# Diagonal masks of the first token group by GpSimd, biases as rows, one K block a unit later, output blocks in four PSUM tiles

## The chip, the cores and the metric

One core of a Trainium2 chip runs the kernel: PE (TensorE, matrix products into PSUM), DVE (VectorE), ACT (ScalarE), POOL (GpSimd) and SP (SyncE, whose queue issues every DMA here). The metric is the device time of one execution in microseconds; a time is the median of several executions.

## The reference

A block with conditioned layer norms over x of shape [2048, 512]: first sliding-window attention over the tokens (32 heads of 16, a token sees itself and the 255 before it), then an MLP that mixes tokens (2048 to 1792 to 2048 for every one of the 512 features).

```python
mod = (_silu(c) @ w_mod).reshape(c.shape[0], 6, 1, -1)
sa, ca, ga, sb, cb, gb = (mod[:, n] for n in range(6))
h = _layernorm(x) * (1 + ca) + sa
x = x + ga * A(h, wqkv, wo)        # A: softmax of q k / 4 over 0 <= i - j < 256, times v, @ wo
h = _layernorm(x) * (1 + cb) + sb
x = x + gb * B(h, w1, b1, w2, b2)  # B: layer norm again, gelu(w1^T h + b1), then w2^T u + b2
```

The bias b1 has 1792 elements and b2 2048. In the kernel they are wanted as columns: b1FM holds one of 14 columns of 128 for each block of w1's outputs, b2FM one of 16 for each block of 128 tokens.

## The kernel before, in words

The tokens are cut into 16 blocks of 128 and four groups tg of four blocks. After a short head (loads, first layer norm, the first projections) the attention runs over 96 units `u = (tg, hs, ui)`: four groups, eight half sets of four heads, three units that hold the pieces of keys and queries of one half set (`UNITS`). `ul = 3 * hs + ui` is a unit's place in its group. For unit u the order is written out by hand in one loop (lines 641 to 668) and each engine keeps to it: `emit_exp(u, 0)` on ACT, `emit_scores(u + 1)` on PE, then the matmuls of one "group" (a projection, a transposition, a product with wo) that `plan(tg)` lays at this place, `emit_exp(u, 1)`, `emit_mask(u)` on GpSimd, some steps of layer norms on DVE by a budget of microseconds (`run_dve`), the group's evacuation on DVE, and `emit_av(u - 1)`, the product with V, on PE. A group's PSUM tile "dn" has one buffer, so a group starts after the one before has been evacuated. The score tiles pss have three buffers, two for a unit.

Two masks are applied. On the diagonal blocks (`DIAG`) PE adds -1e9 from `maskD` to the scores, with four matmuls against `identity` at the end of `emit_scores` (line 435). On the far blocks (`FAR`) GpSimd sets the exponentials to zero with `affine_select` (line 457). In group 0 the first unit of a half set (ui = 0) has one block only, its diagonal, and no far mask.

A K projection (`qk_group` with kind "k") is cast by DVE to `ks`, a tile with one buffer (line 265). In group 0 DVE makes the even and odd halves of its first two blocks itself; for all others eight DMAs of 16 KB copy rows of ks into KT (line 275), so the next cast into ks waits until these have landed. `plan` lays the K projections of blocks 2 and 3 of group 0 at ul 5 and 8, the first two of group 1 at ul 18 and 22 of group 0.

All DMAs stand in SP's queue in the order of the program. `later_loads(n)` is called at ul 10 to 17 of group 0: two blocks of zeros for KT, four blocks of wmod, wod, and with n = 7 the two biases, loaded element by element into [128, 14] and [128, 16] tiles (lines 165 and 166). At ul 16 of group 1 DVE casts them to float32 (lines 627, 628), and the space is then used for w1, whose loads follow.

After the attention PE runs the MLP: the first product (lines 717, 804), gelu on ACT, the second product (line 824). For each of four groups of tokens the second product goes into one PSUM tile py of four banks; the last group is ordered by block tl, the others by fc. DVE then makes o1 (line 831) and the output (line 836) of each block, and SP stores it.

Of the kernel before, what the change touches and what calls it, by code (L numbers as in the profile page):

```python
# [8 lines left out]
DT = mybir.dt  # L9
# [3 lines left out]
P = 128  # L13
# [15 lines left out]
def kernel(  # L29
# [52 lines left out]
    bc_gb = const.tile([P, D], DT.bfloat16, name="bc_gb")  # L82
    b1FM = const.tile([P, NF], DT.float32, name="b1FM")
    b2FM = const.tile([P, NT], DT.float32, name="b2FM")

# [17 lines left out]
    c4 = modw.tile([ND, P], DT.bfloat16, name="c4")  # L103
    b1b = modw.tile([P, NF], DT.bfloat16, name="b1b")
    b2b = modw.tile([P, NT], DT.bfloat16, name="b2b")
    sT_rep = modw.tile([P, ND, P], DT.bfloat16, name="sT_rep")
# [44 lines left out]
    nc.gpsimd.memset(ones[:, 1:2], 0.0)  # L151

    def later_loads(n):
        if n < 2:
            dma.dma_start(
                out=Kring[1 + n][:].rearrange("p g n t -> p (g n) t"),
                in_=zero[:].unsqueeze(1).to_broadcast([P, 2 * ND, 4 * P]),
            )
        elif n < 6:
            v = (2, 4, 3, 5)[n - 2]  # L160
            dma.dma_start(out=wmod[:, :, v * D : (v + 1) * D], in_=w_mod_v[:, :, v * D : (v + 1) * D])
        elif n == 6:
            dma.dma_start(out=wod[:], in_=wo_v[:])
        elif n == 7:
            dma.dma_start(out=b1b[:], in_=B_b1.rearrange("(j p) -> p j", p=P))
            dma.dma_start(out=b2b[:], in_=B_b2.rearrange("(j p) -> p j", p=P))

# [110 lines left out]
    def bc_group(v, dst, add1, pool):  # L278
# [14 lines left out]
        return mms, evac, 0.7  # L293

    folded = []
    done = set()
# [30 lines left out]
    with tc.manual_schedule():  # L327
# [86 lines left out]
        def pieces(tg, ui):  # L414
            return [(4 * tg + kb, r0, nr, blk) for kb, r0, nr, blk in UNITS[ui] if 4 * tg + kb >= 0]

        def emit_scores(u):

# [4 lines left out]
            for n, (kb, r0, nr, blk) in enumerate(pieces(tg, ui)):  # L423
                Ksel = (KeT if par == 0 else KoT)[kb // 4][g8]
                k0, q0 = kb % 4 * P, (kb + r0 - 4 * tg) * P
                for j in range(4):
                    rows = slice(32 * j, 32 * j + 32)
                    nc.tensor.matmul(  # L428
                        pss[j // 2][:, j % 2, blk * P : (blk + nr) * P],
                        lhsT=Ksel[rows, k0 : k0 + P], rhs=QT[tg][g8][rows, q0 : q0 + nr * P],  # L430
                        start=(n == 0), stop=False, tile_position=(32 * j, 0), skip_group_check=True,
                    )
            lo, hi = DIAG[ui]
            for j in range(4):
                nc.tensor.matmul(  # L435
                    pss[j // 2][:, j % 2, lo * P : hi * P], lhsT=identity[:],
                    rhs=maskD[:, 0 : hi - lo, :], start=False, stop=True, skip_group_check=True,
                )
# [12 lines left out]
        def emit_mask(u):  # L451
            tg, hs, ui = units[u]
            if tg == 0 and ui == 0:
                return
            et = state[u, "e"]
            lo, hi = FAR[ui]
            nc.gpsimd.affine_select(  # L457
                out=et[:, :, lo * P : hi * P], in_=et[:, :, lo * P : hi * P],
                pattern=[[0, 4], [0, hi - lo], [-1, P]], compare_op=ALU.is_ge, fill=0.0,
                base=-1, channel_multiplier=1,  # L460
            )

# [119 lines left out]
        def plan(tg):  # L582
# [6 lines left out]
            for n in range(1, 4):  # L589
                lay(n - 1, v_group(tg, n, ps_dn))  # L590
            own = ((3, 1, "k"), (4, 1, "q"), (5, 2, "k"), (6, 2, "q")) if tg == 0 else (
                (3, 1, "q"), (4, 2, "k"), (5, 2, "q"))
            for ul, g8, kind in own + ((8, 3, "k"), (9, 3, "q")):
                lay(ul, qk_group(tg, g8, kind, ps_dn))
            if tg == 1:
                for ul, (v, dst, add1) in zip((6, 7, 10, 15), BC):
                    lay(ul, bc_group(v, dst, add1, ps_dn))
                then[6] = [(lambda g=g: fold_wod(g), 0.45, 0) for g in range(ND)]
# [20 lines left out]
        def at_unit(tg, ul, u):  # L619
# [6 lines left out]
            if tg == 1 and ul == 16:  # L626
                nc.vector.tensor_copy(out=b1FM[:], in_=b1b[:])
                nc.vector.tensor_copy(out=b2FM[:], in_=b2b[:])
                modw.release()
# [184 lines left out]
    with tc.tile_pool(name="ftmp", bufs=3) as ftmp, tc.tile_pool(  # L814
        name="ps_y0", bufs=1, space=bass.MemoryType.PSUM
    ) as ps_y0, tc.tile_pool(name="ps_y1", bufs=1, space=bass.MemoryType.PSUM) as ps_y1:
        for tg in range(NT // 4):
            py = (ps_y0, ps_y1)[tg % 2].tile([P, 4, D], DT.float32, name="py")
            order = [(fc, tl) for fc in range(NF) for tl in range(4)]
            if tg == NT // 4 - 1:  # L820
                order.sort(key=lambda x: x[1])
            for fc, tl in order:
                tb = tg * 4 + tl
                nc.tensor.matmul(  # L824
                    py[:, tl, :], lhsT=w2r[:, fc, tb * P : (tb + 1) * P], rhs=guT[fc][:],
                    start=(fc == 0), stop=(fc == NF - 1),
                )
            for tl in range(4):
                tb = tg * 4 + tl
                o1 = ftmp.tile([P, D], DT.bfloat16, name="o1")  # L830
                nc.vector.scalar_tensor_tensor(  # L831
                    out=o1[:], in0=py[:, tl, :], scalar=b2FM[:, tb : tb + 1], in1=bc_gb[:],
                    op0=ALU.add, op1=ALU.mult,
# [35 lines left out]
```

## Time and profile before

| what | value |
|---|---|
| median of 3 runs | 318.99 us (317.1 to 320.08) |
| profiled execution | 318.7 us |
| its span (first to last instruction) | 317.0 us |
| PE busy | 279.4 us (88%) |
| DVE busy | 198.3 us (63%) |
| ACT busy | 194.8 us (61%) |
| POOL busy | 108.8 us (34%) |
| mean granted clock of PE | 0.979 |

The profile is of one execution. Times in it run from the first instruction. A busy share is an average over the whole span: ACT works mostly in the attention (up to about 215 us) and little after it, PE in both, so the stages are read one by one. A granted clock of 1.00 means 2.4 GHz, 0.50 means 1.2 GHz. In a row of the order of time, the bracket at the end gives how long the engine stood idle before the instruction and what released it.

### The profile page before, as it was taken

The numbers are of one execution on the slowest core, as the hardware profiler recorded it, in microseconds if no ns is written. First come the engines' busy times: TensorE is split into PE (matmuls) and PEld (weight loads), VectorE is DVE, ScalarE is ACT, GpSimd is POOL, SyncE is SP. The second block draws the span as 40 slices with busy tenths as digits, with TensorE's granted clock in tenths as the row PEclk, the third lists the DMA queues.
The fourth block names the chain that finished last, engine by engine and source line by source line (L and its number), as shares of the span: only waits on it lengthen the run. The fifth ranks groups of instructions, "written<-read, shape, count | busy, mean of one in ns | idle before, by whom it ended". The sixth has DMA issues, their size and how long they took to land. (4 is left out here: it accounts for less than half of the span.)

```text
span 317.0 us, 7541 instructions
## 1 busy us (share of the span) xinstructions
PE 279.4 (88%) x3125; PEld 133.2 (42%) x3125; DVE 198.3 (63%) x391; ACT 194.8 (61%) x220; POOL 108.8 (34%) x181
## 2 busy tenths in 40 slices
PE   0899689669999989988888998998999999999991
PEld 0544354324545434444444444443444444444440
DVE  5656594306797789988899998997951100405315
ACT  8177688746999997989989799993106311000000
POOL 5132242222355545537665546772620000000000
PEclk9999999957999999999999999999999999999998
DMA  6910049700000346800000000009990000012011
GB/s 202 345 51 0 22 149 311 160 19 15 17 20 3 123 128 202 295 19 9 2 17 19 6 20 16 2 4 312 417 405 24 1 2 0 13 54 68 17 50 66
DMA packets 23307, 28.55 MB, mean 90 GB/s; under 512 B 6888, under 2 KB 18920, under 8 KB 23272
## 3 DMA queue, kind: packets, MB, share of 16 engines
q1 hardware_dynamic: 23272, 28.07, 27.1%
q8 instruction: 24, 0.39, 0.5%
q14 instruction: 11, 0.09, 0.1%
HBM read 22.03 MB, written 2.10 MB: 76 GB/s over the span
## 5 line engine op out<-in xcount | busy, mean ns | idle before, releaser
L446 ACT ACTIVATE et<-pss 128x1024 bf16<-128x1024 f32 (+1 forms) x192 | 172.8, 971 | 24.6 <-PE pss L435 21.9
L457 POOL TENSOR_SCALAR_AFFINE_SELECT et<-et 128x512 bf16<-128x512 bf16 (+1 forms) x88 | 72.0, 818 | 86.8 <-ACT et L446 86.6
L428 PE MATMUL pss<-QT,KT 32*128 32x256 bf16 (+1 forms) x960 | 44.6, 247 | 10.7 <-ACT et L446 6.6
L824 PE MATMUL py<-guT,w2r 128*128 128x512 bf16 x224 | 48.5, 379 | 0.0
L435 PE MATMUL pss<-maskD,identity 128*128 128x128 bf16 (+1 forms) x384 | 45.8, 243 | 0.0
L831 DVE SCALAR_TENSOR_TENSOR o<-py,b2FM,bc_gb 128x512 bf16<-128x512 f32 x16 | 11.3, 746 | 47.9 <-PE py L824 47.9
L474 PE MATMUL po<-et,VaugT 128*32 128x256 bf16 (+1 forms) x960 | 37.9, 252 | 1.3 <-DVE t L488 1.2
L250 PE MATMUL dn<-h1T,wqkv 128*128 128x512 bf16 x128 | 34.3, 394 | 5.3 <-DVE ks L265 2.9
L824 PEld LDWEIGHTS <-w2r 128*128 128x128 bf16 x224 | 21.9, 98 | 26.4
L428 PEld LDWEIGHTS <-KT 32*128 32x128 bf16 x960 | 18.4, 92 | 31.4 <-issue 22.8
L435 PEld LDWEIGHTS <-identity 128*128 128x128 bf16 x384 | 24.7, 98 | 16.0 <-issue 12.1
L474 PEld LDWEIGHTS <-VaugT 128*32 128x32 bf16 x960 | 16.2, 95 | 35.1 <-issue 24.9
L180 POOL TENSOR_TENSOR ln_rstd<-ln_ve,mhalf 128x1 f32<-128x1 f32 (+1 forms) x40 | 24.6, 616 | 3.3
L488 DVE STREAM_TRANSPOSE t<-po 128x512 f32<-128x512 f32 x32 | 22.6, 706 | 2.2 <-PE po L474 2.2
L265 DVE CAST ks<-dn 128x512 bf16<-128x512 f32 x16 | 11.1, 691 | 20.2 <-DMA KT<-ks 12.4
L176 POOL TENSOR_SCALAR ln_ve<-ln_mv 128x1 f32<-128x1 f32 (+1 forms) x40 | 9.8, 246 | 34.7 <-DVE ln_mv L517 13.6
L230 PE MATMUL dn<-wqkv,h1T 128*128 128x512 bf16 x64 | 18.9, 423 | 2.6 <-DVE ks L265 1.5
L250 PEld LDWEIGHTS <-wqkv 128*128 128x128 bf16 x128 | 12.1, 100 | 15.3 <-issue 8.0
L717 PE MATMUL pu<-hb,w1a 128*128 128x512 bf16 x72 | 16.2, 379 | 0.8 <-ACT et L446 0.8
L241 DVE CAST VaugT<-dn 128x512 bf16<-128x512 f32 x15 | 10.3, 685 | 9.7 <-PE dn L230 7.1
L804 PE MATMUL pu<-hb,w1a 128*128 128x512 bf16 x64 | 14.5, 379 | 0.0
L262 DVE CAST QT<-dn 128x512 bf16<-128x512 f32 x15 | 10.3, 685 | 5.2 <-PE dn L250 5.1
(93 smaller groups left out, 267.3 us busy)
## 6 DMA issues: line engine op xcount, KB each, us to landing
w2r<-in_B_w_dram SPq DMA_DIRECT2D x14, 512.0 KB, 10.1
w1a<-in_B_w_dram SPq DMA_DIRECT2D x12, 448.0 KB, 5.2
wmod<-in_w_mod_dram SPq DMA_DIRECT2D x6, 512.0 KB, 8.2
x<-in_A_x_dram SPq DMA_DIRECT2D x16, 128.0 KB, 2.8
KT<-zero SPq DMA_DIRECT2D x2, 1024.0 KB, 8.4
out_dram<-otile SPq DMA_DIRECT2D x16, 128.0 KB, 1.7
KT<-ks SPq DMA_DIRECT2D x112, 16.0 KB, 1.8
w1b<-in_B_w_dram SPq DMA_DIRECT2D x4, 448.0 KB, 6.1
```

The source lines that it names most:

```text
L180: nc.gpsimd.tensor_tensor(out=r[:], in0=ve[:], in1=mhalf[:, 0:n], op=ALU.pow)
L230: nc.tensor.matmul(pv[:], lhsT=h1T[tg][:, dc, tl * P : (tl + 1) * P], rhs=wqkv[:, dc, 2 * D : 3 * D], start=(dc == 0), stop=(dc == ND - 1),)
L250: nc.tensor.matmul(pq[:], lhsT=wqkv[:, dc, col0 : col0 + P], rhs=h1T[tg][:, dc, :], start=(dc == 0), stop=(dc == ND - 1),)
L428: nc.tensor.matmul(pss[j // 2][:, j % 2, blk * P : (blk + nr) * P], lhsT=Ksel[rows, k0 : k0 + P], rhs=QT[tg][g8][rows, q0 : q0 + nr * P], ...
L435: nc.tensor.matmul(pss[j // 2][:, j % 2, lo * P : hi * P], lhsT=identity[:], rhs=maskD[:, 0 : hi - lo, :], start=False, stop=True, skip_gr ...
L446: nc.scalar.activation(out=et[:, 2 * a : 2 * a + 2, b0 * P :], in_=state.pop((u, a))[:, :, b0 * P :], func=ACT.Exp, scale=SCORE_SCALE,)
L457: nc.gpsimd.affine_select(out=et[:, :, lo * P : hi * P], in_=et[:, :, lo * P : hi * P], pattern=[[0, 4], [0, hi - lo], [-1, P]], compare_o ...
L474: nc.tensor.matmul(po[32 * j : 32 * j + 32, q0 : q0 + nr * P], lhsT=VaugT[kb // 4][:, kb % 4, 8 * g8 + 2 * j + par, :], rhs=et[:, j, blk * ...
L488: nc.vector.transpose(out=state["t2"][:, hs % 2, :], in_=state["po"][:])
L717: nc.tensor.matmul(pu[:, i, :], lhsT=w1_of(sc, fc), rhs=hb[sc][:], start=(sc == 0), stop=(sc == NT - 1),)
L804: nc.tensor.matmul(pu[:, i, :], lhsT=w1_of(sc, fc), rhs=hb[sc][:], start=(sc == s0), stop=(sc == NT - 1),)
L824: nc.tensor.matmul(py[:, tl, :], lhsT=w2r[:, fc, tb * P : (tb + 1) * P], rhs=guT[fc][:], start=(fc == 0), stop=(fc == NF - 1),)
```

## The change

Four edits. In group 0, in units with ui 0 or 1 (`late_diag`), the four mask matmuls are left out, the last score matmul closes the sum, and `emit_mask` runs a second `affine_select` on the diagonal block with the sign turned. The biases are loaded as 14 and 16 rows of 128 elements at the start, behind the loads of x; PE transposes these 30 rows as a group at ul 10 of group 0 and DVE copies the result to float32. In every group the projections of block 3 change places: Q at ul 8, K at ul 9. And each output block gets a PSUM tile of its own: two pools of four tiles of one bank, in place of two tiles of four banks.

```diff
-    b1FM = const.tile([P, NF], DT.float32, name="b1FM")
-    b2FM = const.tile([P, NT], DT.float32, name="b2FM")
+    bFM = const.tile([P, NF + NT], DT.float32, name="bFM")
+    b1FM, b2FM = bFM[:, 0:NF], bFM[:, NF : NF + NT]
...
+    b12 = modw.tile([NF + NT, P], DT.bfloat16, name="b12")
...
+    dma.dma_start(out=b12[0:NF, :], in_=B_b1.rearrange("(j p) -> j p", p=P))
+    dma.dma_start(out=b12[NF:, :], in_=B_b2.rearrange("(j p) -> j p", p=P))
...
-        elif n == 7:
-            dma.dma_start(out=b1b[:], in_=B_b1.rearrange("(j p) -> p j", p=P))
-            dma.dma_start(out=b2b[:], in_=B_b2.rearrange("(j p) -> p j", p=P))
...
+    def bias_group(pool):
+        def mms():
+            pb = pool.tile([P, NF + NT], DT.bfloat16, name="dn")
+            nc.tensor.transpose(pb[:], b12[:], identity[0 : NF + NT, 0 : NF + NT])
+            return pb
+
+        def evac(pb):
+            nc.vector.tensor_copy(out=bFM[:], in_=pb[:])
+        return mms, evac, 0.2
...
+        def late_diag(u):
+            tg, hs, ui = units[u]
+            return tg == 0 and ui < 2
...
-                        start=(n == 0), stop=False, tile_position=(32 * j, 0), skip_group_check=True,
+                        start=(n == 0), stop=late_diag(u) and n + 1 == len(pieces(tg, ui)),
+                        tile_position=(32 * j, 0), skip_group_check=True,
...
-            for j in range(4):
+            for j in range(0 if late_diag(u) else 4):
...
-            if tg == 0 and ui == 0:
-                return
             et = state[u, "e"]
-            lo, hi = FAR[ui]
-            nc.gpsimd.affine_select(
-                out=et[:, :, lo * P : hi * P], in_=et[:, :, lo * P : hi * P],
-                pattern=[[0, 4], [0, hi - lo], [-1, P]], compare_op=ALU.is_ge, fill=0.0,
-                base=-1, channel_multiplier=1,
-            )
+            for (lo, hi), sign, on in ((FAR[ui], -1, (tg, ui) != (0, 0)), (DIAG[ui], 1, late_diag(u))):
+                if on:
+                    nc.gpsimd.affine_select(
+                        out=et[:, :, lo * P : hi * P], in_=et[:, :, lo * P : hi * P],
+                        pattern=[[0, 4], [0, hi - lo], [sign, P]], compare_op=ALU.is_ge, fill=0.0,
+                        base=min(sign, 0), channel_multiplier=-sign,
+                    )
...
-            for ul, g8, kind in own + ((8, 3, "k"), (9, 3, "q")):
+            for ul, g8, kind in own + ((8, 3, "q"), (9, 3, "k")):
                 lay(ul, qk_group(tg, g8, kind, ps_dn))
+            if tg == 0:
+                lay(10, bias_group(ps_dn))
...
-                nc.vector.tensor_copy(out=b1FM[:], in_=b1b[:])
-                nc.vector.tensor_copy(out=b2FM[:], in_=b2b[:])
                 modw.release()
...
-        name="ps_y0", bufs=1, space=bass.MemoryType.PSUM
-    ) as ps_y0, tc.tile_pool(name="ps_y1", bufs=1, space=bass.MemoryType.PSUM) as ps_y1:
+        name="ps_y0", bufs=4, space=bass.MemoryType.PSUM
+    ) as ps_y0, tc.tile_pool(name="ps_y1", bufs=4, space=bass.MemoryType.PSUM) as ps_y1:
         for tg in range(NT // 4):
-            py = (ps_y0, ps_y1)[tg % 2].tile([P, 4, D], DT.float32, name="py")
+            pys = [(ps_y0, ps_y1)[tg % 2].tile([P, D], DT.float32, name="py") for tl in range(4)]
...
-                    py[:, tl, :], lhsT=w2r[:, fc, tb * P : (tb + 1) * P], rhs=guT[fc][:],
+                    pys[tl][:], lhsT=w2r[:, fc, tb * P : (tb + 1) * P], rhs=guT[fc][:],
...
-                    out=o1[:], in0=py[:, tl, :], scalar=b2FM[:, tb : tb + 1], in1=bc_gb[:],
+                    out=o1[:], in0=pys[tl][:], scalar=b2FM[:, tb : tb + 1], in1=bc_gb[:],
```

## Rows read from the trace of the kernel before

**Rows 1.** ACT in order of time: start, duration, line, operation, count, idle before.
```profile
36.12 1.94 ACT L446 ACTIVATE et<-pss 128x1024 bf16<-128x1024 f32 x2 [0.98 <-PE pss L435]
40.12 2.49 ACT L446 ACTIVATE et<-pss 128x1024 bf16<-128x1024 f32 x4 [2.06 <-PE pss L435]
...
58.26 3.83 ACT L446 ACTIVATE et<-pss 128x1024 bf16<-128x1024 f32 x4 [0.98 <-PE pss L435]
65.62 1.94 ACT L446 ACTIVATE et<-pss 128x1024 bf16<-128x1024 f32 x2 [3.53 <-PE pss L435]
...
72.91 1.94 ACT L446 ACTIVATE et<-pss 128x1024 bf16<-128x1024 f32 x2 [3.25 <-PE pss L435]
75.97 4.84 ACT L446 ACTIVATE et<-pss 128x1024 bf16<-128x1024 f32 x5 [1.12 <-PE pss L435]
```

**Rows 2.** PE in order of time, 61 to 70 us.
```profile
61.24 0.34 PE L428 MATMUL pss<-QT,KT 32*128 32x256 bf16 x8
64.50 0.69 PE L428 MATMUL pss<-QT,KT 32*128 32x128 bf16 x4 [2.92 <-DMA KT<-ks]
...
69.32 1.01 PE L230 MATMUL dn<-wqkv,h1T 128*128 128x512 bf16 x2 [1.48 <-DVE ks L265]
```

**Rows 3.** DVE in order of time, 53 to 72 us.
```profile
53.74 0.69 DVE L265 CAST ks<-dn 128x512 bf16<-128x512 f32 x1 [2.18 <-PE dn L250]
...
68.58 0.69 DVE L265 CAST ks<-dn 128x512 bf16<-128x512 f32 x1 [9.20 <-DMA KT<-ks]
```

**Rows 4.** SP's queue in order of time, 43 to 66 us.
```profile
43.01 2.59 SPq L155 DMA_DIRECT2D KT<-zero  x2
...
50.89 1.50 SPq L163 DMA_DIRECT2D wod<-in_A_wo_dram  x1
52.43 1.33 SPq L165 DMA_DIRECT2D b1b<-in_B_b_dram  x1
53.80 6.56 SPq L166 DMA_DIRECT2D b2b<-in_B_b_dram  x1
60.47 5.45 SPq L275 DMA_DIRECT2D KT<-ks  x8
```

**Rows 5.** Stretches: busy time of each engine, granted clock, DMA share, GB/s.
```profile
20.00:60.00 40.00, 33.91 (x493) 17.26 (x493) 26.40 (x50) 31.52 (x43) 12.32 (x20) 1.00 0.43 126
...
64.90:74.90 10.00, 8.44 (x66) 3.20 (x67) 3.05 (x5) 5.82 (x6) 1.77 (x2) 0.50 0.08 18
```

**Rows 6.** DMA issues: count, KB each, median us from issue to landing.
```profile
KT<-ks SPq DMA_DIRECT2D x112, 16.0 KB, 1.8
...
wod<-in_A_wo_dram SPq DMA_DIRECT2D x1, 512.0 KB, 10.2
```

**Rows 7.** DMA packets from 59 to 60 us.
```profile
DMA packets 1327, 0.04 MB, mean 36 GB/s; under 512 B 1294, under 2 KB 1327, under 8 KB 1327
```

**Rows 8.** All engines in order of time, 30 to 56 us.
```profile
30.29 0.40 PE L435 MATMUL pss<-maskD,identity 128*128 128x128 bf16 x4
...
30.53 1.03 PE L250 MATMUL dn<-h1T,wqkv 128*128 128x512 bf16 x4
...
37.26 0.69 DVE L265 CAST ks<-dn 128x512 bf16<-128x512 f32 x1 [3.24 <-DMA KT<-ks]
...
38.01 1.02 PE L250 MATMUL dn<-h1T,wqkv 128*128 128x512 bf16 x4 [1.87 <-DVE ks L265]
```

**Rows 9.** All engines in order of time, from 296 us to the end.
```profile
295.68 14.41 PE L824 MATMUL py<-guT,w2r 128*128 128x512 bf16 x66
...
310.12 1.41 DVE L831 SCALAR_TENSOR_TENSOR o<-py,b2FM,bc_gb 128x512 bf16<-128x512 f32 x2 [8.02 <-PE py L824]
...
313.44 0.75 DVE L836 TENSOR_TENSOR otile<-o,x 128x512 bf16<-128x512 bf16 x2
```

**Rows 10.** Groups by line and shape: count, busy us, mean ns, idle before.
```profile
L457 POOL TENSOR_SCALAR_AFFINE_SELECT et<-et 128x512 bf16<-128x512 bf16 x64 | 45.4, 710 | 61.6 <-ACT et L446 61.5
...
L521 DVE TENSOR_SCALAR hb<-h,ln_mv,ln_rstd 128x512 bf16<-128x512 bf16 x12 | 7.0, 587 | 0.0
...
L754 DVE TENSOR_SCALAR hb<-h,ln_mv,ln_rstd 128x512 bf16<-128x512 bf16 x4 | 1.6, 390 | 0.8 <-POOL ln_rstd L180 0.8
```

More of the change, by code (lines that the diff above doesn't have):

```diff
@@ L103 @@
     c4 = modw.tile([ND, P], DT.bfloat16, name="c4")
-    b1b = modw.tile([P, NF], DT.bfloat16, name="b1b")
-    b2b = modw.tile([P, NT], DT.bfloat16, name="b2b")
+    b12 = modw.tile([NF + NT, P], DT.bfloat16, name="b12")
     sT_rep = modw.tile([P, ND, P], DT.bfloat16, name="sT_rep")
```

## The prediction, made before the changed kernel was run

> **What bounds the kernel now.** I read the busy time by stretch first, then ACT's order of time, and went from each of ACT's waits to the engine and queue behind it. From 17.8 us, where the first exponential starts, to about 215 us the kernel is attention: ACT's exponentials (1.94 us for a full unit) set the pace, with PE just behind. From there to 310 us PE runs matmuls without a gap, and what happens earlier shifts this part as a whole. So a gain counts where ACT waits, or behind the last matmul.
>
> ACT's waits stand where token group 0 passes into group 1. The last unit of group 0 ends at 62.09 (58.26 + 3.83), the next exponential starts at 65.62, and three units then take 10.35 us, to 75.97, where 3 x 1.94 = 5.82 would do [rows 1]. That is 3.53 + 4.53 = 8.06 us lost. The cause can be followed in four steps. PE had the first eight score matmuls of unit 24 done at 61.58 and then waited 2.92 us for a copy into KT [rows 2]. DVE stood for 9.20 us before a ks cast, because ks has one buffer and eight copies still read it; PE's next projection, queued behind it, came only at 69.32 [rows 2, 3]. Those copies were issued at 60.47, though the cast was done at 54.43: SP was busy with b2b until 60.36 [rows 3, 4]. And from 64.9 to 74.9 PE had a granted clock of 0.50 (1.2 of 2.4 GHz), against 1.00 from 20 to 60 [rows 5], after its 2.92 us of idleness.
>
> Bias loads are element by element: 3.5 and 4.0 KB, yet 1294 of the 1327 packets between 59 and 60 us are under 512 B [rows 7]. They come in that stretch although b1b was issued at 52.43, so the rings work in order, and what was issued ahead (two zero blocks of 1 MB, four wmod blocks of 0.5 MB, wod) goes first.
>
> A smaller copy of the same stall lies at unit 8: DVE waits 3.24 us for KT copies before a ks cast [rows 8], and ACT loses 2.06 us behind it [rows 1]. At the end, all four output blocks of the last group start only after the last matmul (310.09), although the order by tl finishes the first block some nine microseconds earlier; DVE then works until 314.19 [rows 9].
>
> **The biases as rows.** Removed: b1b and b2b, 7.9 us of SP's queue [rows 4], and two small DVE casts (at most 0.4 us, beside other work). Added: two loads of 30 rows of 256 B, behind the x loads at about 16 us, where SP has nothing more until 30 us; one PE transpose and one DVE copy at unit 10, some 0.4 us together, and a turn of the single dn buffer. In a unit whose only group is that I take 0, at most 0.4.
>
> What becomes late next? The KT copies of group 1 can now be issued when wod's issue ends, 52.4, instead of 60.5. But in the rings they still stand behind the bulk. wod landed 10.2 us after its issue began, at 61.1 [rows 4, 6]. A KT copy alone takes 1.8 us [rows 6], some of it before its data move, so it lands between 0.1 and 1.8 us behind wod. So the stall shrinks and does not vanish. The start of the bulk is tied to the third K block's copies: SP reaches the zero blocks after them. They need ks, thus the second block's copies, which land about 0.5 us earlier (below). Bulk and wod then land about 0.5 us earlier, at 60.6, and KT between 60.7 and 62.4, say 61.3. Some 0.4 us from score to exponential puts unit 24's first exponential at 61.7 instead of 65.62: minus 3.9, bounds minus 4.5 and minus 2.8. How much faster group 0 itself becomes does not matter for this, which is why I trust it.
>
> The Trainium skill says the same of the rings (DMA: Bandwidth & Descriptors, Queues, rings and completion order: each engine consumes descriptors in ring order); it speaks against this part, since without such an order the result would be rival (b)'s, and the late bias packets agree with it.
>
> After 61.3 the second wait is gone: the eight copies of ks are all issued by about 58, so ks is free at about 61.5 and not 68.58, and PE's projections follow at once. What is left is the clock. PE's idle time becomes 61.3 less the moment at which the first scores of unit 24 are done: 61.58 now, less what group 0 gains. I put that gain at 3.5 us (below), so PE is idle for some 3.2 us, and the nearest row, 2.92 us, was followed by the half clock. I take a dip, but a shorter one, since the second idle time of PE inside it, before 69.32, is gone. At the half clock one unit took 3.06 us (72.91 to 75.97). With 2.1 for the first unit and 2.0 to 3.06 and 3.06 for the next two, unit 27 starts 7.2 to 8.2 us after 61.7, say at 69.4. Now it is 75.97: minus 6.6 in all.
>
> **The third K block a unit later.** The wait of 3.24 us needs 1.9 to 2 us more room, and one unit gives that; with PE quicker, some 0.5 to 0.8 us of it stays. ACT gets back most of the 2.06 us. In groups 1 to 3 no ks cast waits for its copies at this place, so the exchange costs nothing there; the block is needed at unit 17, eight units or 15 us later, and eight copies take 5.45 us to issue [rows 4]. What is behind it on SP is the bulk, as counted above.
>
> **The diagonals by GpSimd.** PE loses four matmuls per unit in 16 units. From the first of them to the next projection is 0.24 us (30.29 to 30.53) [rows 8]; 16 x 0.24 = 3.8 us is the upper bound, and about 0.5 us is gained by unit 5 on the chain that starts the second block's copies. In all group 0 gains about 2 us from the exchange and 1.5 us from the diagonals. This 3.5 us is hidden by the bulk: without that cover it would count in full, and the price of covering it is the longer idle of PE.
> GpSimd gets 16 selects of 0.71 us [rows 10], 11.4 us, in a stretch of 40 us of which it was busy for 12.3 [rows 5]. Per three units it then has 4 x 0.71 = 2.8 us beside about 5 us of ACT. A unit with two selects is ready 0.7 us later; its product with V stands on PE behind the scores of two units on, and these wait 0.97 us for the next half unit's exponential. Bounds: 0, and 8 x 0.3 = 2.4 us, all of it under the bulk's cover; I take 0.
>
> **Output blocks in their own PSUM tiles.** Of the last four blocks, three can be finished under PE. After 310.09 remain one 0.75 us step and one or two of 0.4 us, 1.2 to 1.6 us instead of 4.1: minus 2.5 to 2.9, I take 2.6. Nothing else waits there.
>
> **Sum.** The profiled execution took 318.7 us (span 317.0 and 1.7 around it), 0.3 below the median of 318.99. 318.7 - 6.6 - 2.6 = 309.5.
>
> **Rivals.**
> (a) The clock holds. PE's idle falls across what came before and after differently, and group 0 gains less than I think, so the idle is shorter than 2.9. Then three units take 6.0 us, unit 27 starts at 67.7, and the time is 318.7 - 8.3 - 2.6 = 307.8. Against it: the 2.92 us row. For it: the next 10 us have no second gap, and a wait of 1.87 us ahead of 38.01 left the clock at 1.00 [rows 5, 8].
> (b) The copies overtake the bulk, or the bulk ends sooner without 3840 small packets behind it. Then only group 0's pace counts: unit 24 at 58.6 to 59.5, no dip, 305 to 306.
> (c) Part of the change does nothing: the output blocks still wait for the last matmul (they wait now, and I only argue that the shared tile is why), or the dip lasts ten microseconds and unit 27 starts at 71.5. Either gives 311.5 to 312.
> (d) Slower: GpSimd becomes the bound of group 0. It would have to push unit 27 past 75.97 + 2.6, that is, make three units of group 0 last about 6.9 us, which takes 1.7 us for each of four selects, 2.4 times the 0.71 shown. What could do that is sharing with DVE: the same tensor_scalar into hb took 587 ns beside selects and 390 ns without them [rows 10], so the two do slow each other, by half and not by 2.4. From that factor on the time is 319 and, at 2.0 us a select, 329.
> The Trainium skill describes this sharing as an exclusive lock (SBUF — State Buffer, Who interferes with whom): a GpSimd instruction and a DVE one in a two-port mode block each other for a whole instruction. By it each select could wait for one 0.4 us step, 16 x 0.4 = 6.4 us more on GpSimd, an estimate, still short of (d).
>
> **Chances.** Forecast 0.45, (a) 0.30, (b) 0.08, (c) 0.13, (d) 0.04. The range takes in (a), (b)'s upper half and (c)'s 312, with 1 us for the spread between runs: 305.3 to 313.3. A measurement of this kernel can tell about 1% from no change: faster means below 315.8, and all of the forecast, (a) and (b) and most of (c) lie there, 0.92; within 1% 0.05; slower 0.03.
>
> **What would show it.** On SP wod followed by KT copies at about 52; ACT's wait before unit 24 close to 3 us, released by a KT copy; no ks wait over 5 us; the clock at 0.50 for less than ten microseconds around 62 to 70 (at 1.00 throughout: (a)); two selects per middle unit in group 0 at about 0.7 us; the first three output blocks under PE's last 9 us. Wrong would be a KT copy landing long before or after wod, selects over 1 us, or the o steps still at the end.

## The result, and the profile after

The changed kernel takes 308.71 us (median of four runs, 308.53 to 309.2) against 318.05 for the kernel before: a ratio of 0.970, 95% interval 0.964 to 0.977. The forecast was 309.5, range 305.3 to 313.3. The profiled execution took 308.53 us, span 306.8, against 318.7 and 317.0. Here and below a ratio leaves out an execution that took over 1.5% longer than the fastest of its kernel; there is one, of 314.76 us, among those of the biases as rows alone.

The 10.17 us between the two profiled executions can be laid out along the way to the end. I read the profile after in the order of the forecast: ACT's waits first, then who released them.

ACT in order of time, changed kernel (start, duration, line, operation, count, idle before):
```profile
36.95 2.49 ACT L461 ACTIVATE et<-pss 128x1024 bf16<-128x1024 f32 x4 [0.17 <-PE pss L450]
...
55.88 3.83 ACT L461 ACTIVATE et<-pss 128x1024 bf16<-128x1024 f32 x4 [0.56 <-PE pss L442]
62.37 3.77 ACT L461 ACTIVATE et<-pss 128x1024 bf16<-128x1024 f32 x4 [2.67 <-PE pss L450]
67.64 5.76 ACT L461 ACTIVATE et<-pss 128x1024 bf16<-128x1024 f32 x6 [1.49 <-PE pss L450]
...
120.02 15.29 ACT L461 ACTIVATE et<-pss 128x1024 bf16<-128x1024 f32 x16 [0.40 <-PE pss L450]
135.62 16.96 ACT L461 ACTIVATE et<-pss 128x1024 bf16<-128x1024 f32 x18 [0.30 <-PE pss L450]
```
The kernel before, same view:
```profile
126.39 13.36 ACT L446 ACTIVATE et<-pss 128x1024 bf16<-128x1024 f32 x14 [0.40 <-PE pss L435]
140.59 1.94 ACT L446 ACTIVATE et<-pss 128x1024 bf16<-128x1024 f32 x2 [0.84 <-POOL et L457]
```
Against [rows 1]: unit 24 starts at 62.37, not 65.62, although its wait is still 2.67 us. The row at 67.64 is unit 26, so unit 27 starts at 67.64 + 1.94 = 69.58, not 75.97: 6.39 us gained. The wait of 2.06 us in unit 8 is gone. The long row at 120.02 matters too: it runs through the unit before which the kernel before had a wait of 0.84 us, at 140.59, and now there is none.

PE in order of time, changed kernel:
```profile
58.85 0.34 PE L442 MATMUL pss<-QT,KT 32*128 32x256 bf16 x8
61.24 0.82 PE L442 MATMUL pss<-QT,KT 32*128 32x128 bf16 x4 [2.04 <-DMA KT<-ks]
...
64.04 1.91 PE L229 MATMUL dn<-wqkv,h1T 128*128 128x512 bf16 x4
```
SP's queue in order of time, changed kernel:
```profile
42.62 2.01 SPq L157 DMA_DIRECT2D KT<-zero  x2
44.68 6.22 SPq L163 DMA_DIRECT2D wmod<-in_w_mod_dram  x4
50.94 2.86 SPq L165 DMA_DIRECT2D wod<-in_A_wo_dram  x1
53.91 7.61 SPq L274 DMA_DIRECT2D KT<-ks  x8
```
DVE in order of time, changed kernel:
```profile
51.77 0.69 DVE L264 CAST ks<-dn 128x512 bf16<-128x512 f32 x1 [1.65 <-DMA KT<-zero]
...
62.80 0.69 DVE L264 CAST ks<-dn 128x512 bf16<-128x512 f32 x1 [5.94 <-DMA KT<-ks]
```
Beside [rows 2] the same wait of PE stands there, released by the same tile, 3.3 us earlier (61.24 instead of 64.50). Beside [rows 4], wod is followed at once by the KT copies: they are issued from 53.91, not 60.47, and yet the first of them lands 7.3 us later, at 61.2, where 1.8 us is the median of all [rows 6]: they still stand in the rings (the queues of transfers already issued) behind wod. Beside [rows 3], ks waits 5.94 us and not 9.20; PE's next projection follows at 64.04 with no wait of its own, so in this trace the wait no longer costs anything.

Stretches of the changed kernel (us; busy time and count of PE, PEld, DVE, ACT, POOL; granted clock; DMA share; GB/s):
```profile
38.00:51.00 13.00, 11.49 (x150) 5.75 (x151) 8.85 (x20) 10.57 (x16) 8.43 (x15) 0.74 0.55 164
...
62.00:64.00 2.00, 1.49 (x25) 0.77 (x25) 0.69 (x1) 1.63 (x2) 0.00 (x0) 0.99 0.03 8
64.00:66.00 2.00, 2.00 (x16) 0.60 (x16) 0.01 (x1) 2.00 (x3) 1.10 (x1) 0.50 0.08 18
66.00:68.00 2.00, 2.00 (x30) 1.04 (x27) 1.93 (x4) 0.51 (x2) 0.68 (x1) 0.66 0.12 29
68.00:70.00 2.00, 2.00 (x34) 1.08 (x33) 1.75 (x4) 1.97 (x3) 0.29 (x1) 1.00 0.11 26
```
The half clock behind the stall lasts from about 64 to 67.4 us; it fell 2.8 us after PE's wait had ended at 61.24. Before, it held from 64.9 to 74.9 [rows 5]. The first row is new: within 38 to 51 us the clock was 1.00 before and is 0.74 now.

All engines at the end, changed kernel:
```profile
295.65 7.29 PE L838 MATMUL py<-guT,w2r 128*128 128x512 bf16 x33
...
299.95 0.75 DVE L845 SCALAR_TENSOR_TENSOR o<-py,bFM,bc_gb 128x512 bf16<-128x512 f32 x1 [1.81 <-PE py L838]
...
302.98 0.75 DVE L845 SCALAR_TENSOR_TENSOR o<-py,bFM,bc_gb 128x512 bf16<-128x512 f32 x1 [1.81 <-PE py L838]
303.76 0.42 DVE L850 TENSOR_TENSOR otile<-o,x 128x512 bf16<-128x512 bf16 x1
```
The first output blocks are finished while PE still runs. PE's last matmul ends at 295.65 + 7.29 = 302.94 and DVE at 303.76 + 0.42 = 304.18: 1.24 us behind it, where [rows 9] had 4.10. That gains 2.86.

The sum: 6.39 (unit 27) + 0.84 (the wait at 140.59) + 2.86 (the end) = 10.09 of 10.17 us.

The selects, by line and shape, changed kernel (count, busy us, mean ns, idle before):
```profile
L471 POOL TENSOR_SCALAR_AFFINE_SELECT et<-et 128x512 bf16<-128x512 bf16 x80 | 56.2, 709 | 45.6 <-ACT et L461 45.4
```
There are sixteen more of them, at the same mean as in [rows 10], 709 instead of 710 ns; PE waited for GpSimd twice, 0.7 us in all. The exclusive lock that I quoted from the Trainium skill (SBUF — State Buffer, Who interferes with whom) lengthened no select that this mean would show.

### The profile page after: what moved, and what is told of

Read it like the earlier page. It is cut to its first block, busy times and chain, and to the rows that moved or that the text cites. A ratio compares the mean times of both kernels' runs of the same rounds, so it can differ in the third digit from the quotient of the medians.

```text
span 306.8 us, 7438 instructions
## 1 busy us (share of the span) xinstructions
PE 274.4 (89%) x3062; PEld 129.4 (42%) x3062; DVE 200.3 (65%) x390; ACT 194.9 (64%) x220; POOL 119.7 (39%) x197
## 5 line engine op out<-in xcount | busy, mean ns | idle before, releaser
L471 POOL TENSOR_SCALAR_AFFINE_SELECT et<-et 128x512 bf16<-128x512 bf16 (+1 forms) x104 | 83.0, 803 | 68.7 <-ACT et L461 68.4
L442 PE MATMUL pss<-QT,KT 32*128 32x256 bf16 (+1 forms) x960 | 43.1, 248 | 8.7 <-ACT et L461 6.1
L845 DVE SCALAR_TENSOR_TENSOR o<-py,bFM,bc_gb 128x512 bf16<-128x512 f32 x16 | 11.4, 746 | 44.3 <-PE py L838 44.3
L450 PE MATMUL pss<-maskD,identity 128*128 128x256 bf16 (+1 forms) x320 | 39.6, 247 | 0.0
L450 PEld LDWEIGHTS <-identity 128*128 128x128 bf16 x320 | 20.9, 98 | 13.8 <-issue 10.4
```

What stands on the lines that cost most here:

```text
L442: nc.tensor.matmul(pss[j // 2][:, j % 2, blk * P : (blk + nr) * P], lhsT=Ksel[rows, k0 : k0 + P], rhs=QT[tg][g8][rows, q0 : q0 + nr * P], ...
L450: nc.tensor.matmul(pss[j // 2][:, j % 2, lo * P : hi * P], lhsT=identity[:], rhs=maskD[:, 0 : hi - lo, :], start=False, stop=True, skip_gr ...
L471: nc.gpsimd.affine_select(out=et[:, :, lo * P : hi * P], in_=et[:, :, lo * P : hi * P], pattern=[[0, 4], [0, hi - lo], [sign, P]], compare ...
```

## The experiments

Theory 1 is that of the forecast: what stands in the DMA rings ahead of group 1's first KT copies (the bulk, the 4.5 MB of zero blocks, wmod and wod, and in the kernel before the two bias loads) sets the start of unit 24, and PE's idle time there brings the half clock. The rival, theory 2: group 0's own pace sets it, through the exchanged K block and the diagonals, and the bias loads are a side matter. Each kernel was timed in turns with the kernel before on the same chip, in three groups of four on three chips. The kernel before took 317.48 us beside rows alone, tiles alone, exchange undone and diagonals undone; 317.61 beside element-wise biases, bulk early, bulk early with both undone and 14 matmuls; 318.09 beside the other four. Across groups the ratios are the safer comparison.

### Biases as rows, alone

The kernel before with this one part of the change; masks, order of the K blocks and output tiles as they were.
```diff
-    dma.dma_start(out=b1b[:], in_=B_b1.rearrange("(j p) -> p j", p=P))   # at n == 7
-    dma.dma_start(out=b2b[:], in_=B_b2.rearrange("(j p) -> p j", p=P))
...
+    dma.dma_start(out=b12[0:NF, :], in_=B_b1.rearrange("(j p) -> j p", p=P))
+    dma.dma_start(out=b12[NF:, :], in_=B_b2.rearrange("(j p) -> j p", p=P))
...
+    lay(10, bias_group(ps_dn))
...
```


> The kernel before with the biases as rows alone (row loads, one transpose and one copy at unit 10; masks, third K block and output tiles as before). Theory 1, the bulk loads in the rings set when unit 24 starts: unit 24 at about 62 instead of 65.6, the next three units in 6 to 8 us, so 312 to 313 from a before of 318. Theory 2, group 0's own pace sets it: the 2 to 3.5 us of the diagonals and the exchange are missing as well, so 314 to 315.5.

Measured: 311.54 us, ratio 0.979 [0.976, 0.982], 6.7 us less by the ratio (5.9 by the medians).

ACT in order of time, and then one row of PE, kernel before with the biases as rows:
```profile
58.37 3.83 ACT L461 ACTIVATE et<-pss 128x1024 bf16<-128x1024 f32 x4 [0.98 <-PE pss L450]
62.62 3.77 ACT L461 ACTIVATE et<-pss 128x1024 bf16<-128x1024 f32 x4 [0.41 <-PE pss L450]
```
```profile
65.61 1.86 PE L229 MATMUL dn<-wqkv,h1T 128*128 128x512 bf16 x4 [1.20 <-DVE ks L264]
```
Unit 24 starts at 62.62, 3.0 us earlier than in [rows 1], although group 0 is no faster than before (its last two units start at 58.37, before 58.26). ACT's wait is down to 0.41 us: here the KT copies are in time, and the end of group 0, at 62.20, sets the start. The profiled execution took 314.76 us and the other five 309.76 to 312.0, so I take only this order of events from it. PE still waits 1.20 us for a ks cast behind it and runs at half clock from about 64.5 to 71.3; the other five executions had a mean granted clock of 0.993 to 0.996 against 0.985, so they stood less at half clock; no trace shows where. This one edit carries most of the gain, as theory 1 says.

### Output tiles, alone

```diff
-            py = (ps_y0, ps_y1)[tg % 2].tile([P, 4, D], DT.float32, name="py")
+            pys = [(ps_y0, ps_y1)[tg % 2].tile([P, D], DT.float32, name="py") for tl in range(4)]
```


> The kernel before with the output blocks in four PSUM tiles alone. Theory 1: the first three blocks of the last group are finished under PE, 2.5 to 2.9 us less behind the last matmul, 315.2 from a before of 318. Rival, the steps wait for something else at the end: no change.

Measured: 314.82 us, ratio 0.991 [0.989, 0.993], 2.9 us less by the ratio (2.7 by the medians). The end of its trace has the shape of the changed kernel's.

All engines at the end, kernel before with four output tiles:
```profile
309.98 0.75 DVE L831 SCALAR_TENSOR_TENSOR o<-py,b2FM,bc_gb 128x512 bf16<-128x512 f32 x1 [1.81 <-PE py L824]
310.76 0.42 DVE L836 TENSOR_TENSOR otile<-o,x 128x512 bf16<-128x512 bf16 x1
```
One step of 0.75 and one of 0.42 us are left behind the last matmul: it was the shared tile that made all four blocks wait. Unit 24 starts at 65.21, as before.

### The biases element by element again

The changed kernel with b1b and b2b behind wod again; the row loads and their transposition are left out, and DVE casts the two tiles as before.
```diff
...
+        elif n == 7:
+            dma.dma_start(out=b1b[:], in_=B_b1.rearrange("(j p) -> p j", p=P))
+            dma.dma_start(out=b2b[:], in_=B_b2.rearrange("(j p) -> p j", p=P))
...
```


> The changed kernel with the biases loaded element by element at unit 17 again. Theory 1: the copies of group 1 go out at about 60 as in the kernel before, unit 27 starts near 75.5, and only the tail is gained: 314.5 to 316. Theory 2, the diagonals and the exchange carry part of the gain: 311 to 313.

Measured: 312.86 us, ratio 0.984 [0.981, 0.987].

PE, and then ACT, in order of time, changed kernel with element-wise biases:
```profile
64.38 0.66 PE L444 MATMUL pss<-QT,KT 32*128 32x128 bf16 x4 [6.68 <-DMA KT<-ks]
```
```profile
54.38 3.83 ACT L463 ACTIVATE et<-pss 128x1024 bf16<-128x1024 f32 x4 [0.56 <-PE pss L444]
65.46 1.94 ACT L463 ACTIVATE et<-pss 128x1024 bf16<-128x1024 f32 x2 [7.25 <-PE pss L452]
...
71.02 44.68 ACT L463 ACTIVATE et<-pss 128x1024 bf16<-128x1024 f32 x46 [1.50 <-PE pss L452]
```
This is the sharpest test of the two theories. Group 0 ends at 58.2 us here (its last units start at 54.38), 3.9 us earlier than before, and unit 24 still starts at 65.46, against 65.62 before. A faster group 0 only makes the wait longer, 7.25 us on ACT. As to the start of unit 24, theory 2 falls.

By its time alone this run would speak for theory 2, though: 312.86 us lies in theory 2's range (311 to 313) and below theory 1's (314.5 to 316). The stretches say why (columns as above):
```profile
60.00:62.00 2.00, 0.00 (x0) 0.00 (x0) 0.00 (x0) 0.00 (x0) 0.00 (x0) 0.50 0.55 9
...
68.00:70.00 2.00, 2.00 (x16) 0.55 (x14) 0.24 (x1) 1.52 (x2) 0.97 (x2) 0.50 0.07 16
70.00:72.00 2.00, 2.00 (x32) 0.94 (x28) 1.93 (x4) 0.98 (x2) 0.33 (x1) 0.94 0.10 25
```
The clock fell while PE was still idle, and was back soon after 70 us, not at 75. Part of the half clock lay in time that was lost anyway: unit 26 starts at 71.02 instead of 72.91 and unit 27 at 72.96 instead of 75.97. So the faster group 0 did gain 3.0 us here, not by an earlier unit 24 but by where the half clock fell.

### The bulk early

The changed kernel, with the bulk loads issued before attention starts and not between units 10 and 17.
```diff
...
+        for n in range(7):
+            later_loads(n)
...
-            if tg == 0 and 10 <= ul < 18:
-                later_loads(ul - 10)
```


> The changed kernel with its seven bulk loads (two zero blocks, four wmod blocks, wod) issued behind the bias rows at about 17 us, where SP is idle until 30, and not at units 10 to 16. Theory 1, the copies of group 1's first K block wait behind the bulk in the rings: unit 24 starts when group 0 ends, at about 59.5, no ks wait at unit 22, no half clock around 65: 3 to 4.5 us less than the changed kernel, 304 to 305.5. Rival, the copies are late because SP issues them one by one or because ks has one buffer: 307.5 to 308.5.

Measured: 304.48 us, ratio 0.958 [0.955, 0.961]: 4.2 us below the changed kernel.

SP's queue in order of time, bulk early:
```profile
16.50 1.44 SPq L157 DMA_DIRECT2D KT<-zero  x2
17.99 6.44 SPq L163 DMA_DIRECT2D wmod<-in_w_mod_dram  x4
24.48 2.79 SPq L165 DMA_DIRECT2D wod<-in_A_wo_dram  x1
```
ACT in order of time, bulk early:
```profile
55.10 52.36 ACT L464 ACTIVATE et<-pss 128x1024 bf16<-128x1024 f32 x54 [0.56 <-PE pss L445]
```
54 activations run from group 0's last two units far into group 1 without a wait: once the rings are empty, the stall at unit 24 is gone. The rival named above, that SP's issuing one by one or the single buffer of ks makes the copies late, would have left 307.5 to 308.5 us; a ks cast does still wait for copies here (2.53 us before 58.63), and ACT loses nothing by it. The KT copies issued from 50 to 60 us land 1.8 to 2.7 us after their issue (medians by stretch), where the first one of the changed kernel's needed 7.3 behind the bulk. That agrees with the ring order of the Trainium skill (DMA: Bandwidth & Descriptors, Queues, rings and completion order).

### The bulk early, without the exchange and the diagonals

With the rings out of the way these two edits should show their own worth. Three kernels: bulk early with both undone, with only the exchange undone, with only the diagonals undone.
```diff
-            for ul, g8, kind in own + ((8, 3, "q"), (9, 3, "k")):
+            for ul, g8, kind in own + ((8, 3, "k"), (9, 3, "q")):     # exchange undone
...
-            return tg == 0 and ui < 2
+            return False                                              # diagonals on PE again
```


> The same early bulk loads, with the diagonals on PE and the third K block at unit 8 as before the change. Theory 1: without the bulk's cover group 0's pace counts in full, so this is 2 to 4 us slower than the early bulk with both edits: 307 to 309. If both edits are worth nothing anywhere: equal to it.

> Early bulk loads with the third K block at unit 8. Theory, without the bulk's cover the exchange counts in group 0 (about 2 us), and the ks waits in groups 1 and 2 come on top (0.3 to 2 us): 306 to 307.5 against 304.5.

> Early bulk loads with all diagonals on PE. Theory, without the bulk's cover the 64 matmuls count where PE leads, 1.5 to 2 us: 305.8 to 306.8 against 304.5. Rival, they count in full with 3.8 us or more: above 308.

Measured: both undone 308.84 us, ratio 0.971 [0.967, 0.974]; exchange undone 309.79, 0.974 [0.971, 0.978]; diagonals undone 304.02, 0.957 [0.954, 0.960].

The exchange is worth 5.3 us here (304.48 against 309.79), more than I had expected, and 4.8 with the diagonals on PE (304.02 against 308.84). By ACT's rows, from the first exponential to unit 22: 37.56 us with it (17.54 to 55.10) and 40.25 without (17.90 to 58.15), so 2.7 in group 0. The rest comes later. ACT, and then DVE, in order of time in group 2, bulk early without the exchange:
```profile
133.44 1.94 ACT L464 ACTIVATE et<-pss 128x1024 bf16<-128x1024 f32 x2 [1.71 <-PE pss L453]
```
```profile
130.58 0.69 DVE L264 CAST ks<-dn 128x512 bf16<-128x512 f32 x1 [1.63 <-DMA KT<-ks]
```
The third K block's cast waits for the copies of the block before in group 2 too, and ACT behind it; two smaller waits stand at 83.66 (0.28 us, of which ACT loses 0.15) and 185.90 (0.74). With the exchange, none of these three waits is there. With 0.36 us of a later first exponential, which is no work of the exchange, the pieces give 2.7 + 0.36 + 0.15 + 1.7 + 0.7 = 5.6, and the profiled executions differ by 309.28 - 303.68 = 5.6.

The diagonals on GpSimd are worth nothing here: 304.48 with them, 304.02 without, and with the exchange undone 309.79 with them, 308.84 without. I had expected 1.5 to 2 us. In the two profiled executions group 0 does gain 0.9 us, 37.56 against 38.44 from the first exponential to unit 22, and the one with GpSimd had started its first exponential 0.74 us later; the medians, of four executions each, show no gain. Stretches of bulk early, and of bulk early with the diagonals on PE:
```profile
38.00:51.00 13.00, 11.16 (x160) 5.87 (x164) 8.96 (x20) 11.42 (x18) 8.98 (x15) 0.87 0.05 13
```
```profile
38.00:51.00 13.00, 11.53 (x187) 6.41 (x189) 8.51 (x20) 11.56 (x18) 5.19 (x9) 1.00 0.05 13
```
PE has fewer matmuls in the first, and nearly the same busy time, since part of the stretch runs at the lower clock.

### Single parts undone with the bulk where it was

The changed kernel with the exchange undone, and with the diagonals undone (the same one-line edits).

> The changed kernel with the third K block back at unit 8. Theory 1: the ks cast waits for the second block's copies until about 36.8 us either way, so the bulk starts at 42.6 as before and unit 24 at 62.4; ACT loses some 2 us in group 0 that the wait at unit 24 gives back: 308.5 to 309.3. Theory 2, group 0's pace counts: 310 to 311.

> The changed kernel with all diagonal masks added by PE. Theory 1: the second K block's copies and the bulk come some 0.5 us later, the rest is under the bulk: 308.7 to 309.5. Theory 2, the 64 matmuls count at 0.24 us per unit or more: 310 to 312. Rival, GpSimd's selects cost more than they give: under 308.

Measured: exchange undone 310.01 us (307.23 to 311.1), ratio 0.975 [0.972, 0.978]; diagonals undone 311.24 (309.47 to 312.27), ratio 0.979 [0.976, 0.982]. Both times are longer than theory 1 gave (308.5 to 309.3, and 308.7 to 309.5) and lie in theory 2's ranges; the traces show that neither got there by theory 2's way.

Without the exchange there is no stall at unit 24 at all. ACT in order of time, exchange undone:
```profile
40.16 2.49 ACT L461 ACTIVATE et<-pss 128x1024 bf16<-128x1024 f32 x4 [3.80 <-PE pss L450]
...
59.06 25.23 ACT L461 ACTIVATE et<-pss 128x1024 bf16<-128x1024 f32 x26 [0.56 <-PE pss L442]
...
134.78 1.94 ACT L461 ACTIVATE et<-pss 128x1024 bf16<-128x1024 f32 x2 [1.92 <-PE pss L450]
```
Group 0 ends at 62.9, when the KT copies have landed, so units 22 to 27 run through, at a clock of 1.00, and unit 27 starts at 59.06 + 5 x 1.94 = 68.8, 0.8 us earlier than in the changed kernel. It loses that, and 1.3 us more, in groups 1 and 2: 1.92 us before 134.78, 0.51 before 84.79. Theory 1 had left these waits out.

Without GpSimd's diagonals the bulk starts at 44.30, not 42.62, the KT copy releases PE at 62.26 after 2.49 us, and unit 24 starts at 63.46, 1.1 us later. Stretches, diagonals undone:
```profile
38.00:51.00 13.00, 11.20 (x177) 6.46 (x177) 9.48 (x21) 11.52 (x17) 5.87 (x10) 1.00 0.47 148
62.00:75.00 13.00, 11.61 (x115) 4.98 (x117) 5.14 (x10) 7.48 (x8) 2.45 (x3) 0.61 0.05 13
```
ACT in order of time, diagonals undone:
```profile
73.33 42.71 ACT L461 ACTIVATE et<-pss 128x1024 bf16<-128x1024 f32 x44 [1.29 <-PE pss L450]
```
Now group 0 keeps its clock, and behind the stall the half clock lasts from 62.3 to 72.6; unit 27 starts at 73.33, not 69.58.

### Matmuls in PE's idle time

Matmuls into a score tile that the next scores overwrite, ahead of unit 24's: 14, then 9, then 9 with the diagonals undone.
```diff
...
+            if u == 24:
+                for n in range(9):          # 14 in the first
+                    nc.tensor.matmul(
+                        pss[0][:, 0, :], lhsT=identity[:], rhs=wqkv[:, 0, 0 : 4 * P], start=True, stop=True,
+                        skip_group_check=True,
+                    )
...
```


> The changed kernel with 14 extra matmuls of 512 columns (3 us at 2.4 GHz) on PE ahead of unit 24's scores, into a PSUM region that the scores then overwrite, so that PE isn't idle while it waits for the KT copies. Theory: the half clock after 64 us comes from that idle time; without it units 25 and 26 lose nothing: 1.0 to 1.7 us less than the changed kernel, 307 to 307.5. Rival, the ks wait alone makes the loss: no change, or 0.5 us more.

> The changed kernel with 9 extra matmuls of 512 columns (some 2.0 us) ahead of unit 24's scores, not 14: those ended at 62.6, behind the arrival of the KT copies, and made unit 24 0.9 us late. Theory, the half clock after 64 us comes from PE's idle time and costs the 1.49 us that ACT waits before unit 26: unit 24 at 62.4 as in the changed kernel, clock 1.00 from 60 to 70, 1.0 to 1.5 us less, 307.2 to 307.7. Rival, the loss is in the order of the work and not in the clock: no change.

> The changed kernel with all diagonals on PE again and the same 9 extra matmuls ahead of unit 24. Theory, what the diagonals on PE cost there (2.5 us) is 1.1 us of a later bulk and, for the rest, a half clock of 10.2 us in place of 3.4: with PE kept busy the clock stays at 1.00 and the time is 308.5 to 309.5. Rival, the 64 matmuls themselves cost the 2.5 us: 311 to 311.5.

Measured: 14 matmuls 308.55 us, ratio 0.971 [0.968, 0.975]; nine 306.84, 0.966 [0.963, 0.968]; nine with the diagonals undone 308.27, 0.970 [0.967, 0.974].

The first gave nothing by the medians (308.55 against 308.71), by its own doing: the 14 ended at 62.6, and unit 24 started at 63.27. Nine fit. ACT in order of time, and then a stretch, nine matmuls:
```profile
61.74 48.63 ACT L467 ACTIVATE et<-pss 128x1024 bf16<-128x1024 f32 x50 [2.51 <-PE pss L456]
```
```profile
62.00:75.00 13.00, 12.28 (x187) 5.94 (x187) 9.91 (x17) 12.79 (x14) 5.01 (x6) 1.00 0.06 14
```
ACT still waits 2.51 us before unit 24, but PE works for 2.12 us of its wait: the clock stays at 1.00, and units 24 to 27 follow without a wait. All five runs (306.0 to 307.75) lie below the four of the changed kernel (308.53 to 309.2), which were not timed beside it; by the ratios the gain is 1.5 us, by the medians 1.9. In the traces unit 27 starts 2.0 us earlier, and 0.6 of that was there before the extra matmuls could matter: this execution's unit 24 starts at 61.74, its first exponential at 16.85 and not 17.35. That leaves 1.4 us for the clock.

With the diagonals undone the nine matmuls take the stretch from 0.61 to 1.00 and the ratio from 0.979 to 0.970, about 2.7 us. So the half clock behind the stall comes from PE's idle time. It makes up about 1.1 of the 2.5 us that undoing the diagonals costs: with the nine matmuls in both, the diagonals on PE still cost 1.4 us (308.27 against 306.84, same chip). Unit 24 starts later there.

ACT in order of time, nine matmuls and diagonals undone:
```profile
62.79 48.63 ACT L467 ACTIVATE et<-pss 128x1024 bf16<-128x1024 f32 x50 [3.11 <-PE pss L456]
```
That is 1.05 us behind the 61.74 above, 0.42 of it a later first exponential.

## Why the prediction was right, point by point

- **What bounds the kernel.** Right. Unit 24's start follows the rings: 65.2 to 65.6 in the three kernels whose biases come element by element (group 0 ends between 58.2 and 62.2), 61.7 to 63.5 in the seven that load them as rows and keep the bulk where it was, and no wait at all in the four with the bulk early. Three of the seven have caught up with the copies: with rows alone and with the exchange undone group 0's own end (62.2, 62.9) sets the start, with 14 matmuls these do.
- **The biases as rows: unit 24.** Forecast 61.7 with KT at 61.3; measured 62.37 and 61.24. The copy landed as computed, through the bulk's earlier start (42.62 for 43.01), though SP reached the copies at 53.91 and not at 52.4: wod's issue now takes 2.86 us instead of 1.50. The term that was mis-sized is the step from the KT copy to the first exponential, 0.4 us: it was 1.13 (61.24 to 62.37). The rows of before had it, 1.12 us (64.50 to 65.62) [rows 1, 2]; I had not taken it from them. So 3.25 us were gained, not 3.9.
- **The rest up to unit 27.** Forecast 69.4, measured 69.58. The dip came, and shorter, as taken: from unit 24's start to unit 27's it is 7.2 us, forecast 7.7. This makes up for most of the 0.7 above, by luck, so the sum of 6.6 against 6.39 is better than its parts. The dip itself came without the reason given for it: PE was idle for 2.04 us, not some 3.2, so it was less than the 2.92 us of the row that the forecast leaned on, and the clock fell all the same.
- **"No ks wait over 5 us", ks free at about 61.5.** Wrong: it was 5.94 us, with the cast at 62.80. The eight copies were to be issued from 52.4 in 5.45 us; they began at 53.91 and took 7.61. The reason behind it, that PE's projections no longer stand behind that wait, held.
- **The third K block: "in groups 1 to 3 the exchange costs nothing".** This step failed, to the good side. I counted only a possible cost there and took nothing as its value; the place had a wait, 0.84 us at 140.59, that is gone with the exchange. The profile of before does not show its cause by name: PE stands 0.68 us behind a ks cast at 137.74, whose own wait of 0.76 us is put down to a PE matmul. The runs with the block put back name the KT copies (1.84 us before the cast at 131.92 with the exchange undone, 1.63 with the bulk early), and ACT loses 1.9 and 1.7 us there in group 2. The size varies: rows alone have 0.49 us there, tiles alone 0.16, bulk early with both undone 0.27 (and these last two 1.10 and 1.28 in group 1). So the 0.84 of this pair of executions is one draw. In group 0 the 2 us that I gave it are there (37.56 against 40.25 us with the bulk early), and hidden by the bulk, as said: without the exchange unit 27 comes 0.8 us earlier.
- **Group 0 gains 3.5 us.** It gained 2.4 (its last exponential ends at 59.71, not 62.09), and 0.45 of those are an earlier start of the first exponential (17.35 for 17.80). What is missing is the diagonals' 1.5 us: from the first exponential to unit 22 it is 40.46 us before, 38.45 with the diagonals undone and 38.53 in the changed kernel, so the exchange gives its 2 us and the diagonals nothing. The clock fell within 38 to 51 us, which I had not foreseen. Since the bulk covers this, it cost the sum little.
- **The selects.** 0.71 us each, and no bound: right; rival (d) had no support.
- **The end.** Forecast 2.6 us, measured 2.86 in the traces, and 2.7 to 2.9 for that part alone.
- **Rivals.** (a), the clock holds, would have been 307.8. Its condition came true, an idle time shorter than 2.9 us, and what it was to bring did not. The run with nine matmuls is that case made by hand, at 306.84. (b) was not seen: no copy overtook the bulk. What it would have brought is near to what the early bulk gives, 304.5 against its 305 to 306 (its own terms add up to 304.5 to 305.5). (c) was not either, although undoing the diagonals gives its second half, unit 27 at 73.33 and 311.24 us.

The gains of the parts do not add up. The rows and the tiles alone give 6.7 + 2.9 = 9.6 us by the ratios, as much as the whole change (9.4), yet from the whole, undoing the exchange or the diagonals costs 1.3 and 2.5 us by the medians. The traces give the reasons for the direction. The diagonals change when the bulk starts and how the half clock falls behind the stall; the exchange removes the ks waits of groups 1 and 2. The diagonals' worth is thus 2.5 us here, 1.4 with the clock held behind the stall, and nothing that the medians show with the bulk early. How the time would split with the clock held everywhere stays open. Runs of one kernel spread by up to 4 us (307.23 to 311.1 with the exchange undone), and with one trace of each kernel it is not shown where.

A version that beats both kernels came out of the experiments: the changed kernel with the bulk issued before attention, 304.5 us, with the diagonals on either engine.

## What to carry to other kernels

Here a copy that a stage waited for landed behind the 4.5 MB that had been issued ahead of it. Look at what was issued ahead of such a copy, and move loads that nobody needs yet to a time when nobody waits: here that gave 4.2 us on top of the whole change. Before you credit an edit that speeds up a covered stage, ask what lies at the same place in the later rounds, and what the idle time that it makes does to the clock.

## What the runs showed of the hardware that was not expected

Moving work from PE to GpSimd lowered PE's clock. Mean granted clock within 38 to 51 us of the profiled executions:

| diagonals of group 0 | kernels | clock |
|---|---|---|
| on GpSimd | changed; nine matmuls; 14 matmuls; bulk early without exchange | 0.74 each |
| on GpSimd | exchange undone | 0.68 |
| on GpSimd | bulk early; element-wise biases | 0.87 each |
| on PE | before, diagonals undone, the same with nine matmuls, bulk early with diagonals undone or with both undone, rows alone, tiles alone | 1.00 each |

All seven kernels with 64 matmuls fewer in group 0 have stretches at half clock there, and none of the seven others has one. In the changed kernel these lie at about 40 to 43.5 and 47 to 50.3 us. The edit is the only difference within four pairs of these kernels, so it brings the lower clock. It does two things, though: it takes matmuls off PE and it lets PE wait for selects (0.16 to 0.81 us at a time; none of the seven others has such a wait in group 0). In six of the seven the clock first fell before that wait, so the missing matmuls are the likelier reason; no run separates the two. Nor is it a matter of the profiled executions alone: with the bulk early, the mean clock over the whole kernel was 0.988 to 0.994 in all four executions with the diagonals on GpSimd, and 0.999 to 1.000 in the four with them on PE.

The lower clock ate most of what the edit saved. From the first exponential to unit 22 the kernels with the exchange take 37.3 and 37.6 us at a clock of 0.87 (element-wise biases; bulk early), 38.5 to 38.8 at 0.74 (changed; nine matmuls; 14 matmuls), and 38.4 to 38.6 at 1.00 with the diagonals on PE: the edit saves about 1 us where the clock fell less, and nothing where it fell more.

The other way round, nine matmuls that compute nothing, 2.1 us of PE's time, made the kernel about 1.5 us faster, because they stand where PE would have been idle.
